# A recurrent-memory attention kernel: where the first half's row sums and the filler matmuls stand in a segment

## The chip, the cores and the metric

The kernel runs on one core of one Trainium2 chip. The time is device microseconds from start to end of one execution. Three executions of the kernel before took 1645.75, 1645.52 and 1643.44 us, so the median is 1645.52 us. A core has five engines that run side by side and wait for each other by semaphores: PE (TensorE: matmuls; its weight loads are shown apart as PEld), DVE (VectorE), ACT (ScalarE), POOL (GpSimd) and SP (SyncE, which here only issues DMAs). PE reads from SBUF and writes to PSUM, of which there are eight banks of 512 float32 columns.

## The reference, cut to what matters

Two layers, each of an attention block with a recurrent memory (A) and a gated feed-forward block (B), are run twice over 2048 rows of 512 columns. Only A is touched:

```python
mem = mem0                                   # 8 rows
for s in range(n_seg):                       # 2048 / 32 = 64 segments
    xs = x[:, s * seg_len:(s + 1) * seg_len, :]
    h = jnp.concatenate([mem, xs], axis=1)   # 8 + 32 = 40 rows
    q, k, v = (jnp.einsum('btd,dhe->bhte', h, W) for W in (Wq, Wk, Wv))   # 32 heads of 128
    scores = jnp.einsum('bhqe,bhke->bhqk', q, k) * scale
    p = softmax(where(mask, scores, -1e9))
    o = jnp.einsum('bhqk,bhke->bhqe', p, v)
    o = jnp.einsum('bhte,hed->btd', o, Wo)
    mem = o[:, :M, :]                        # the next segment needs these 8 rows
    outs.append(o[:, M:, :])
```

Each segment's memory rows are computed from the segment before, so 64 segments run one after another, in each of two layers: 128 in all. The softmax is not divided out on the scores: the kernel keeps E = exp(scores) times the mask, and divides the product of E and the values by the sums of E over the keys.

## The kernel before, in words

`segment` (L887) emits one segment. The order on PE, DVE and ACT is the order in which the program emits the instructions; POOL and SP are ordered by the framework.

**Heads and halves.** The 32 heads are handled in two halves, r = 0 and 1, of 16 heads each. For each half there are projections of Q and K (`qk`), a cast of the result by ACT (L904), a turn by DVE's 32x32 transposes (L907, into QQ and KA), scores on PE (`scores`, L930 and L934, into psS), an exponential on ACT (`exps`, L939), and a product with the mask on DVE (`close`, L942, into E). E has 128 partitions: four groups of 32 keys, where a group holds every fourth head; the mask writes each score row twice with zeros where another head stands, so that one contraction over 64 partitions serves two groups. The new values are cast to VA by ACT (L1018, half 0) and DVE (L1027, half 1).

**Tiles of the array.** Most matmuls use the array as four tiles of 128 rows and 32 columns (`tile_position=(0, 32 * cg)`), so that four matmuls run side by side, each writing 32 partitions of PSUM. The products with the values (`pv`, L973 and L976, into psO[r]) and the sums (`sums_memory` L956, `sums_tokens` L965) use it as two tiles of 64 rows and 128 columns: g is the pair of key groups on partitions 64g to 64g + 63.

**Sums and outputs.** `sums_memory(r, ps, fresh)` sums E over the keys for the queries that are memory rows: four matmuls with a matrix of ones, two of them over a second part of E that holds the segment-end rows (`e_own`). For r = 0 the sums go to psT (two banks, shared in time with psS and psQ under the tag "att"), for r = 1 to columns 320 to 383 of psO[1]. `memory_out(r, ps)` takes the logarithm (L990) and the exponential of its negative (L991) on ACT into Rm, and DVE multiplies psO[r]'s memory rows by it into uT (L992). `sums_tokens` fills psT with the sums for all other queries, which are inverted later in Rt (L1054, L1057) and used by `tok_out` and `last_out` (L995, L998).

**Wo.** `wo_pairs` (L773, into px) takes heads 0 to 19 from uT and so needs half 0's memory rows first, and half 1's from head 16 on; `wo_rest` (L780) takes heads 20 to 31 into columns 384 to 511 of psO[0]. `fold` and `build_hA` (L869 to L879) add the pieces and turn them into the next segment's first rows of hT, with which its projections (psQ) begin. psQ also waits until Rt's logarithm (L1054) has read psT.

**Fillers.** Work that is off this chain is handed out in pieces by a generator, `more`; `fill()` asks it for the next piece. In three segments of four it is `b_units`: full passes of 16 matmuls (four k-tiles by four column tiles) that project the last 8 rows of each segment of the next 128-row block (hB) into psb. A pair of passes is given out as three pieces: k-tiles 0 to 2 of the first (12 matmuls), its k-tile 3 (4 matmuls), and the whole second pass (16). In the other segment, from the fifth block on, it is `y_part`, a piece of Wo for those rows (pwB), split in the same way; in the first four blocks that segment has no filler. So a layer has four such segments without fillers, eight in all. Finished passes are cast by ACT (L758) and turned by a DMA on SP (L763), both issued by `run(copies)`.

The three calls of `fill()` in a segment stand behind `close(1)`, behind `memory_out(1)`, and behind `last_out(0)`. What PE sees of it is: scores of half 1; 12 filler matmuls; `sums_memory(0)`; `pv(0)`; `pv(1)`; `sums_memory(1)`; `sums_tokens`; 4 filler matmuls; `wo_pairs`; `wo_rest`; 16 filler matmuls; the next segment. The first segment of the first layer takes its fillers elsewhere.

Of the kernel before, what the change touches and what calls it, by code (L numbers as in the profile page):

```python
# [7 lines left out]
BF16 = mybir.dt.bfloat16  # L8
# [6 lines left out]
P = 128  # L15
# [38 lines left out]
def _consts(ctx, tc, c, b_sp):  # L54
    nc = tc.nc
    cp = ctx.enter_context(tc.tile_pool(name="consts", bufs=1))
    bsp = cp.tile([P, 16], F32, name="bsp")
    tctx = ExitStack()
    tmp = tctx.enter_context(tc.tile_pool(name="consts_tmp", bufs=1))
    ident_f = tmp.tile([P, P], F32, name="ident_f")  # L60
    nc.gpsimd.memset(ident_f[:], 0.0)
    nc.gpsimd.affine_select(out=ident_f[:], in_=ident_f[:], compare_op=ALU.not_equal, fill=1.0,
                            base=0, pattern=[[-1, P]], channel_multiplier=1)
    ident_bf = cp.tile([P, P], BF16, name="ident_bf")
    nc.vector.tensor_copy(ident_bf[:], ident_f[:])


    maskf = tmp.tile([P, 224], F32, name="maskf")
    nc.gpsimd.memset(maskf[:], 1.0)
    fourth = tmp.tile([P, 4, 32], F32, name="fourth")  # L70
    nc.gpsimd.memset(fourth[:], 0.0)
    nc.gpsimd.affine_select(out=fourth[:], in_=fourth[:], compare_op=ALU.not_equal, fill=1.0,
                            base=0, pattern=[[-1, 4], [-4, 32]], channel_multiplier=1)
    own = maskf[:, 160:224].rearrange("p (i q) -> p i q", i=4)
    is_own = tmp.tile([P, 4, 1], F32, name="is_own")
    nc.vector.tensor_reduce(out=is_own[:], in_=fourth[:], op=ALU.max, axis=mybir.AxisListType.X)
    nc.vector.tensor_copy(own, is_own[:].to_broadcast([P, 4, 16]))
    for q in range(0, P, 32):
        blk = maskf[q:q + 32, 0:160].rearrange("p (i q) -> p i q", i=4)[:, :, 8:32]
        nc.gpsimd.affine_select(out=blk, in_=blk, compare_op=ALU.is_ge, fill=0.0, base=8,  # L80
                                pattern=[[0, 4], [1, 24]], channel_multiplier=-1)
        last = own[q:q + 32, :, 8:16]
        nc.gpsimd.affine_select(out=last, in_=last, compare_op=ALU.is_ge, fill=0.0, base=0,
                                pattern=[[1, 4], [4, 8]], channel_multiplier=-1)
    maskN = cp.tile([P, 2, 224], BF16, name="maskN")
    nc.vector.memset(maskN[:], 0.0)
    for gs in range(4):
        nc.vector.tensor_copy(maskN[32 * gs:32 * gs + 32, gs % 2, :], maskf[32 * gs:32 * gs + 32, :])
    ones = cp.tile([P, P], BF16, name="ones")
    nc.vector.memset(ones[:], 1.0)  # L90
    bsp_bf = cp.tile([P, 16], BF16, name="bsp_bf")

    def load_bsp():
        nc.vector.memset(bsp_bf[:], 0.0)
        nc.sync.dma_start(bsp_bf[:], b_sp.rearrange("(t p) -> p t", p=P))
        return lambda: nc.vector.tensor_copy(bsp[:], bsp_bf[:])

    c["bsp"], c["load_bsp"] = bsp, load_bsp
    tctx.close()
    c.update(ident_bf=ident_bf, maskN=maskN, ones=ones)  # L100
    return c


# [549 lines left out]
def a_block(tc, c, rows, front, MV_in, RS_in, MV_out, RS_out, ahead, wo, S, first):  # L653
    nc = tc.nc
    NSEG = S // SEG
    NB = S // P
    scale = float(DH) ** -0.5
    maskN, ones = c["maskN"], c["ones"]

    with ExitStack() as ctx:  # L660

# [74 lines left out]
        def b_units(tb, early=0):  # L736
            bs = blk_state[tb]
            order = (0, 2, 1, 3, 4, 5) if early else (4, 5, 0, 2, 1, 3)

            for k, j in enumerate(order):  # L740
                now = k < early
                ps = (accB if now and k % 2 and j != 5 else accA).tile([P, 512], F32, name="psb")[:]
                for kts in (((0, 1, 2), (3,)), ((0, 1, 2, 3),))[k % 2]:
                    mm_chunk(ps, lambda kt, cg: bs["hB"][:, kt, :],
                             lambda kt, cg: qk_rhs(w, j, kt, cg) if j < 4 and now else cols_rhs(w, j, kt, cg), kts)
                    if kts[-1] != KT - 1:
                        yield

                def out(k=k, j=j, ps=ps, now=now):
                    if j >= 4:  # L750
                        nc.scalar.copy(bs["VB"][:, :, j - 4, :], ps.rearrange("p (i e) -> p i e", i=4))
                        if now:
                            ahead.regroup(bs["VB"], bs["VX"], (j - 4,))
                        elif j == 5:
                            store_v(bs)
                        return
                    r = rowsB[:, k % 2, :]
                    nc.scalar.copy(r, ps)  # L758
                    t = bs[("QTB", "KTB")[j // 2]][:, j % 2]
                    if now:  # L760
                        turns.append(lambda: nc.vector.transpose(out=t.rearrange("p a b -> p (a b)"), in_=r))
                    else:
                        nc.sync.dma_start_transpose(out=t.rearrange("p (i g) k -> p i (g k)", g=4), in_=r.rearrange("t (i e) -> t i e", i=4))  # L763

                copies.insert(len(copies) if now else 0, out)
                yield
# [29 lines left out]
        def y_part(G, q, last=False):  # L796

            groups = [oBs[G][:, :, 32 * g:32 * g + 32] for g in range(4)]
            if last:
                parts = [[(groups[g], 8 * q + k) for g in range(3)] + [(groups[q], 24 + k)] for k in range(8)]  # L800
            else:
                parts = [[(groups[g], 8 * q + k) for g in range(4)] for k in range(8)]
            pwB = accA.tile([P, DM], F32, name="pwB")
            for k, _ in enumerate(wo_last(parts, pwB)):
                if k in (2, 3):
                    yield

            def add(lo, n, src):
                nc.vector.tensor_tensor(out=yB[G][lo:lo + n, :], in0=pwB[src:src + n, :], in1=yB[G][lo:lo + n, :], op=ALU.add)

            def out():
                n = 96 if last else P
                if q == 0:
                    yB[G] = wk.tile([P, DM], F32, name="yB", bufs=1)
                    nc.vector.tensor_copy(yB[G][0:n, :], pwB[0:n, :])
                else:
                    add(0, n, 0)
                if last:
                    if q == 2:
                        store_last(G, 0, 64, nc.sync)  # L820
                    add(32 * q, 32, 96)
                    if q == 2:
                        store_last(G, 64, 96, nc.sync)
                elif q == 3 and G < NB // 4 - 2:
                    stores.append(lambda: store_last(G, 0, P, nc.sync))
                elif q == 3:
                    store_last(G, 0, P, nc.sync)

            adds.append(out)
            yield  # L830
# [56 lines left out]
        def segment(s, fill, spare1, spare2, spare3, tail, loads):  # L887
# [11 lines left out]
            E = segp.tile([P, 2, 2, 224], BF16, name="E", bufs=1)  # L899
# [44 lines left out]
            def e_all(e, lo, hi):  # L944

                return e[:, :, 0:160].rearrange("p n (i q) -> p n i q", q=40)[:, :, :, lo:hi]

            def e_own(e, b):
                return e[:, :, 160:224].rearrange("p n (i b e) -> p n i b e", i=4, b=2)[:, :, :, b, :]

            def sums_memory(r, ps, fresh):

                for k in range(2):
                    for g in range(2):
                        e = E[64 * g:64 * g + 64, r]
                        nc.tensor.matmul(ps[:, g, :], lhsT=ones[64 * g:64 * g + 64, :], rhs=e_own(e, 0) if k else e_all(e, 0, 8),  # L956
                                         start=(fresh and k == 0), stop=True, skip_group_check=True)

            def sums_tokens(ps):

# [69 lines left out]
            psO = [attO[r].tile([P, 2, 512], F32, name="psO") for r in range(2)]  # L1030
            Rm = segp.tile([P, 2, 2, 64], F32, name="Rm", bufs=1)
            psT = att.tile([P, 2, 512], F32, name="psT")
            sums = (psT[:, :, 0:64], psO[1][:, :, 320:384])
            if not (first and s == 0):
                fill()
            sums_memory(0, sums[0], True)
            pv(0)
            memory_out(0, sums[0])
            spare1(E)
            pv(1)  # L1040
            sums_memory(1, sums[1], False)
            sums_tokens(psT)
            memory_out(1, sums[1])
            if not (first and s == 0):
                fill()
            run(copies)
            px = accB.tile([P, 512], F32, name="px")
            wo_pairs(px, uT_cur)
# [43 lines left out]
        start = nc.vector if first else nc.gpsimd  # L1092
# [114 lines left out]
        for i in range(H // 2):  # L1207
            for k in range(4):
                h = 2 * i + k % 2
                nc.tensor.matmul(pw[32 * k:32 * k + 32, :], lhsT=ends[k // 2][:, h, :], rhs=wo.head(h).rearrange("p (kt g el) -> p g kt el", kt=4, g=4),  # L1210
                                 start=(i == 0), stop=(i == H // 2 - 1), tile_position=(0, 32 * k))
# [46 lines left out]
```

## Time and profile before

| what | value |
|---|---|
| median of three runs (1643.44 to 1645.75) | 1645.52 us |
| profiled execution, its own time | 1643.32 us |
| its span (first to last instruction) | 1641.6 us |
| granted TensorE clock, mean | 0.997 |
| busy: PE / PEld / DVE / ACT / POOL | 97% / 58% / 74% / 65% / 18% |
| segments, psQ to psQ: usual | 10.10 to 10.20 us |
| segment without fillers | 10.10 us |
| two feed-forward blocks, from the last segment's start on | 159 us, and the span's last 153 us |

The profile is one execution taken by the hardware profiler. The times of all rows are microseconds from the span's start. A matmul's row runs from its start to a modelled end, so rows of PE overlap; the distance between starts tells how long a group takes on the array. A row of weight loads (PEld) can begin ahead of its matmuls. What stands in brackets behind a row is the idle time of the engine ahead of it, and what ended it.

### The profile page before, as it was taken

Reading aid. Unit: us, or ns where it says so; the run is one execution under the profiler, and the core shown is the slowest. Engines: PE = TensorE matmul, PEld = TensorE weight load, DVE = VectorE, ACT = ScalarE, POOL = GpSimd, SP = SyncE. Lnnn points to the kernel's source line nnn. Section 1 sums busy time; section 2 is a strip of 40 time slices with the busy share of each in tenths; the row PEclk is TensorE's granted clock in tenths of the full one; section 3 lists DMA queues with packets and bytes.
Section 4 is the critical chain, followed back from the end, with each engine's and each line's share of the span. In section 5 each row is a group of like instructions: output and inputs, shape, how many; then the busy total and the mean of one; then the engine's idle time right before and its main releaser. Section 6 shows DMA issues by size and latency. Waiting matters only on the chain.

```text
span 1641.6 us, 86352 instructions
## 1 busy us (share of the span) xinstructions
PE 1585.8 (97%) x38610; PEld 953.5 (58%) x38610; DVE 1207.2 (74%) x3176; ACT 1074.9 (65%) x2278; POOL 290.0 (18%) x604
## 2 busy tenths in 40 slices
PE   3899999999999999999999999999999999999999
PEld 1455556555565556566655555665565666565565
DVE  3677777778887887884467777777788778878722
ACT  2577777777777777661047777777777777776400
POOL 5111111112211222320011111111122112214000
PEclk9999999999999999999999999999999999999999
DMA  9322111113321233276952222222233223435697
GB/s 354 101 42 42 42 42 44 44 42 74 81 57 42 76 89 79 87 180 154 215 163 46 50 48 45 46 46 45 57 92 84 46 59 95 100 60 156 150 194 166
DMA packets 264731, 148.99 MB, mean 91 GB/s; under 512 B 198680, under 2 KB 240784, under 8 KB 264360
## 3 DMA queue, kind: packets, MB, share of 16 engines
q1 hardware_dynamic: 251128, 99.66, 27.8%
q0 software_dynamic: 13232, 43.82, 8.3%
q8 instruction: 302, 4.95, 1.3%
q14 instruction: 69, 0.57, 0.1%
HBM read 59.68 MB, written 37.19 MB: 59 GB/s over the span
## 4 chain that ended last, share of the span: by engine, by line
PE 55%; DVE 2%; ACT 1%; issue 0%; DMA 0%; DVEq 0%
PE pg L388 9%; PE psQ L697 7%; PE psK L697 7%; PE psb L697 5%; PE px L773 4%; PE pz L287 4%; PE psV L697 3%; PE psm L697 3%; PE psO L780 2%; PE py L431 2%; PE psO L973 2%; PE pwB L792 1%; PE psT L965 1%; PE psS L930 1%; PE psT L956 1%; PE pw L1210 0%
## 5 line engine op out<-in xcount | busy, mean ns | idle before, releaser
L697 PEld LDWEIGHTS <-hT 128*32 128x32 bf16 x12288 | 328.6, 96 | 318.6 <-DVE hT L879 84.2
L907 DVE STREAM_TRANSPOSE QQ<-rows 128x512 bf16<-128x512 bf16 x256 | 179.5, 701 | 16.8 <-ACT rows L904 11.8
L907 DVE STREAM_TRANSPOSE KA<-rows 128x512 bf16<-128x512 bf16 x256 | 175.3, 685 | 11.5 <-ACT rows L904 8.7
L388 PE MATMUL pg<-z,wspT 128*128 128x344 bf16 x1024 | 154.3, 309 | 0.0
L904 ACT CAST rows<-psQ 128x512 bf16<-128x512 f32 x256 | 140.9, 585 | 17.1 <-PE psQ L697 16.9
L995 DVE TENSOR_TENSOR uT<-psO,Rt 128x384 bf16<-128x384 f32 x256 | 141.1, 551 | 12.4 <-ACT Rt L1057 8.1
L1057 ACT ACTIVATE Rt<-Rt 128x512 f32<-128x512 f32 x256 | 147.2, 622 | 4.1
L697 PE MATMUL psQ<-Wq_sb,hT 128*32 128x512 bf16 x2048 | 135.3, 383 | 11.2 <-ACT Rt L1054 6.0
L939 ACT ACTIVATE S<-psS 128x224 bf16<-128x224 f32 x256 | 91.4, 357 | 81.3 <-PE psS L934 81.2
L992 DVE TENSOR_TENSOR uT<-psO,Rm 128x128 bf16<-128x128 f32 x256 | 74.5, 291 | 93.2 <-ACT Rm L991 85.8
L773 PEld LDWEIGHTS <-uT 128*32 128x32 bf16 x5120 | 125.3, 96 | 26.9 <-DVE uT L992 13.3
L773 PE MATMUL px<-Wo,uT 128*32 128x256 bf16 x3840 | 134.5, 274 | 1.1 <-DMA Wo<-in_A_Wo_dram 0.2
L697 PE MATMUL psQ<-Wk_sb,hT 128*32 128x512 bf16 x2048 | 134.5, 380 | 0.0
L697 PE MATMUL psK<-Wv_sb,hT 128*32 128x512 bf16 x2048 | 134.2, 379 | 0.0
L697 PE MATMUL psm<-Wq_sb,hT 128*32 128x512 bf16 x2048 | 134.2, 379 | 0.0
L697 PE MATMUL psK<-Wk_sb,hT 128*32 128x512 bf16 x2048 | 134.2, 379 | 0.0
L697 PE MATMUL psV<-Wv_sb,hT 128*32 128x512 bf16 x2048 | 133.6, 378 | 0.0
L1054 ACT ACTIVATE Rt<-psT 128x1024 f32<-128x1024 f32 x128 | 131.1, 1024 | 3.2
L388 PEld LDWEIGHTS <-wspT 128*128 128x128 bf16 x1024 | 100.2, 98 | 53.2
L863 POOL COPY KX<-old 128x128 bf16<-128x128 bf16 x128 | 69.1, 548 | 304.5 <-PE psS L934 243.5
L863 POOL COPY KX<-front 128x128 bf16<-128x128 bf16 x126 | 66.8, 546 | 293.7 <-PE psS L934 226.0
L697 PEld LDWEIGHTS <-hB 128*32 128x32 bf16 x2976 | 70.1, 96 | 81.3 <-issue 30.4
(192 smaller groups left out, 2949.4 us busy)
## 6 DMA issues: line engine op xcount, KB each, us to landing
o_d<-o_sb SPq DMA_DIRECT2D x126, 64.0 KB
vb_d<-front SPq DMA_DIRECT2D x30, 256.0 KB
VX<-vb_d SPq DMA_DIRECT2D x120, 64.0 KB
ln_x<-xd SPq DMA_DIRECT2D x26, 256.0 KB
y_o<-o_d POOLq DMA_DIRECT2D x22, 256.0 KB, 3.4
xd<-y_o POOLq DMA_DIRECT2D x22, 256.0 KB, 3.0
Wq_sb<-in_A_Wq_dram POOLq DMA_DIRECT2D x8, 512.0 KB, 9.2
Wk_sb<-in_A_Wk_dram POOLq DMA_DIRECT2D x8, 512.0 KB, 11.0
```

What stands on the lines that cost most here:

```text
L287: nc.tensor.matmul(pz[:, c0:c1], lhsT=xnT[:, kt, :], rhs=w_in_sb[:, kt, c0:c1], start=(kt == 0), stop=(kt == KT - 1))
L388: nc.tensor.matmul(pg[t][:, k, 0:344], lhsT=wsp[t][:, st, :], rhs=z(st, 344 * k, 344 * k + 344), start=(st == 0), stop=(st == NT - 1))
L697: return [nc.tensor.matmul(ps[32 * cg:32 * cg + 32, :], lhsT=lhs(kt, cg), rhs=rhs(kt, cg), start=(kt == 0), stop=(kt == KT - 1), tile_posi ...
L773: nc.tensor.matmul(px[at:at + 32, 0:256], lhsT=lhs[:, h, :], rhs=wo_rhs(h, slice(k + 2, None, -2) if h % 2 else slice(k, None, 2)), start= ...
L863: eng.tensor_copy(KX[:, :, r].rearrange("p g (k i) -> p i g k", i=4), bs["KTB"][:, r].rearrange("p (i g) k -> p i g k", i=4)[:, :, :, 8 * ...
L904: return r, mms, nc.scalar.copy(r[:], ps)
L907: nc.vector.transpose(out=QQ[:, j % 2, :, 0:32] if j < 2 else KA[:, j % 2], in_=r[:])
L939: return nc.scalar.activation(out=S[:, r], in_=psS[:, r, 0:224], func=ACT.Exp, scale=scale)
L992: nc.vector.tensor_tensor(out=hview(uT_cur[:], r, 24, 32), in0=oview(r, 0, 8), in1=rm.rearrange("p g (n q) -> p g n q", q=8), op=ALU.mult)
L995: nc.vector.tensor_tensor(out=hview(uT_nxt[:], r, 0, 24), in0=oview(r, 8, 32), in1=rview(r, 0, 24), op=ALU.mult)
L1054: nc.scalar.activation(out=Rt[:], in_=psT[:], func=ACT.Ln)
L1057: nc.scalar.activation(out=rt, in_=rt, func=ACT.Exp, scale=-1.0)
```

## The change

`sums_memory` now serves half 1 alone. For half 0 there is `sums_ahead`: sixteen matmuls on 128x32 tiles, which is the tile form of the fillers. They contract over all 128 partitions with a constant, `half`, that is one on 64 partitions and zero on the other 64, so that each g gets the same sums as before. They write the two g side by side into columns 384 to 511 of psO[1]'s first bank, and no longer into psT. They are emitted behind the first filler piece and ahead of the second.

The calls of `fill()` stand behind `close(1)`, behind `sums_ahead`, and, as before, behind `last_out(0)`; the one between `memory_out(1)` and `run(copies)` is gone. The first pass is split as k-tile 0 (4 matmuls) and k-tiles 1 to 3 (12), and `y_part` yields at 0 and 3 in place of 2 and 3. So PE sees: scores of half 1; 4 filler matmuls; `sums_ahead` (16 small ones); 12 filler matmuls; `pv(0)`; `pv(1)`; `sums_memory(1)`; `sums_tokens`; `wo_pairs`; `wo_rest`; 16 filler matmuls. The semaphore waits that the changed program has and the one before had not: the first matmul of `sums_ahead` waits for DVE's E of half 0, `pv(1)` waits for ACT's L1003 (the logarithm of half 0's sums, L990 before), and `sums_tokens` no longer waits for that logarithm.

```diff
--- before.py
+++ after.py
@@ -88,6 +88,10 @@
         nc.vector.tensor_copy(maskN[32 * gs:32 * gs + 32, gs % 2, :], maskf[32 * gs:32 * gs + 32, :])
     ones = cp.tile([P, P], BF16, name="ones")
     nc.vector.memset(ones[:], 1.0)
+    half = cp.tile([P, 2, 32], BF16, name="half")
+    nc.vector.memset(half[:], 0.0)
+    for g in range(2):
+        nc.vector.memset(half[64 * g:64 * g + 64, g, :], 1.0)
     bsp_bf = cp.tile([P, 16], BF16, name="bsp_bf")
 
     def load_bsp():
@@ -97,7 +101,7 @@
 
     c["bsp"], c["load_bsp"] = bsp, load_bsp
     tctx.close()
-    c.update(ident_bf=ident_bf, maskN=maskN, ones=ones)
+    c.update(ident_bf=ident_bf, maskN=maskN, ones=ones, half=half)
     return c
 
 
@@ -655,7 +659,7 @@
     NSEG = S // SEG
     NB = S // P
     scale = float(DH) ** -0.5
-    maskN, ones = c["maskN"], c["ones"]
+    maskN, ones, half = c["maskN"], c["ones"], c["half"]
 
     with ExitStack() as ctx:
 
@@ -740,7 +744,7 @@
             for k, j in enumerate(order):
                 now = k < early
                 ps = (accB if now and k % 2 and j != 5 else accA).tile([P, 512], F32, name="psb")[:]
-                for kts in (((0, 1, 2), (3,)), ((0, 1, 2, 3),))[k % 2]:
+                for kts in (((0,), (1, 2, 3)), ((0, 1, 2, 3),))[k % 2]:
                     mm_chunk(ps, lambda kt, cg: bs["hB"][:, kt, :],
                              lambda kt, cg: qk_rhs(w, j, kt, cg) if j < 4 and now else cols_rhs(w, j, kt, cg), kts)
                     if kts[-1] != KT - 1:
@@ -802,7 +806,7 @@
                 parts = [[(groups[g], 8 * q + k) for g in range(4)] for k in range(8)]
             pwB = accA.tile([P, DM], F32, name="pwB")
             for k, _ in enumerate(wo_last(parts, pwB)):
-                if k in (2, 3):
+                if k in (0, 3):
                     yield
 
             def add(lo, n, src):
@@ -948,13 +952,22 @@
             def e_own(e, b):
                 return e[:, :, 160:224].rearrange("p n (i b e) -> p n i b e", i=4, b=2)[:, :, :, b, :]
 
-            def sums_memory(r, ps, fresh):
+            def sums_memory(r, ps):
 
                 for k in range(2):
                     for g in range(2):
                         e = E[64 * g:64 * g + 64, r]
                         nc.tensor.matmul(ps[:, g, :], lhsT=ones[64 * g:64 * g + 64, :], rhs=e_own(e, 0) if k else e_all(e, 0, 8),
-                                         start=(fresh and k == 0), stop=True, skip_group_check=True)
+                                         start=False, stop=True, skip_group_check=True)
+
+            def sums_ahead(ps):
+
+                e = E[:, 0]
+                for g in range(2):
+                    for k in range(2):
+                        for cg in range(4):
+                            nc.tensor.matmul(ps[32 * cg:32 * cg + 32, g, :], lhsT=half[:, g, :], rhs=e_own(e, 0) if k else e_all(e, 0, 8),
+                                             start=(g == 0 and k == 0), stop=True, tile_position=(0, 32 * cg), skip_group_check=True)
 
             def sums_tokens(ps):
 
@@ -1030,19 +1043,19 @@
             psO = [attO[r].tile([P, 2, 512], F32, name="psO") for r in range(2)]
             Rm = segp.tile([P, 2, 2, 64], F32, name="Rm", bufs=1)
             psT = att.tile([P, 2, 512], F32, name="psT")
-            sums = (psT[:, :, 0:64], psO[1][:, :, 320:384])
+            sums = (psO[1][:, 0, 384:512].rearrange("p (g n) -> p g n", g=2), psO[1][:, :, 320:384])
             if not (first and s == 0):
                 fill()
-            sums_memory(0, sums[0], True)
+            sums_ahead(sums[0])
+            if not (first and s == 0):
+                fill()
             pv(0)
             memory_out(0, sums[0])
             spare1(E)
             pv(1)
-            sums_memory(1, sums[1], False)
+            sums_memory(1, sums[1])
             sums_tokens(psT)
             memory_out(1, sums[1])
-            if not (first and s == 0):
-                fill()
             run(copies)
             px = accB.tile([P, 512], F32, name="px")
             wo_pairs(px, uT_cur)
```

## The prediction

> **What bounds the kernel now.** The first view is the page: the engines' busy shares and the chain that ended last.
>
> ```profile
> span 1641.6 us, 86352 instructions
> PE 1585.8 (97%) x38610; PEld 953.5 (58%) x38610; DVE 1207.2 (74%) x3176; ACT 1074.9 (65%) x2278; POOL 290.0 (18%) x604
> PE 55%; DVE 2%; ACT 1%; issue 0%; DMA 0%; DVEq 0%
> ```
>
> PE carries the chain, but "97% busy" is not "97% useful": a matmul's row includes its trip through the array. What counts is when each group of matmuls starts, so the second view is the timeline of one segment, 267.81 to 277.98 us (128 such segments run one after another, nearly all within 10.1 to 10.3 us). Columns: start, duration, engine, line, tile written and read, count.
>
> ```profile
> 272.92 0.39 DVE L942 TENSOR_TENSOR E<-S,maskN 128x448 bf16<-128x448 bf16 x1
> 273.12 0.28 PE L930 MATMUL psS<-QQ,KA 128*32 128x40 bf16 x16
> 273.22 0.21 PE L934 MATMUL psS<-QQ,KX 128*32 128x64 bf16 x4
> 273.25 0.83 PE L697 MATMUL psb<-Wq_sb,hB 128*32 128x512 bf16 x12
> 273.55 0.36 ACT L939 ACTIVATE S<-psS 128x224 bf16<-128x224 f32 x1 [0.19 <-PE psS L934]
> 273.96 0.38 DVE L942 TENSOR_TENSOR E<-S,maskN 128x448 bf16<-128x448 bf16 x1
> 274.01 0.23 PE L956 MATMUL psT<-E,ones 64*128 64x64 bf16 x4
> 274.08 0.31 PE L973 MATMUL psO<-E,VA 64*128 64x80 bf16 x8
> 274.22 0.22 PE L976 MATMUL psO<-E,VX 64*128 64x128 bf16 x2
> 274.40 0.32 PE L973 MATMUL psO<-E,VA 64*128 64x80 bf16 x8
> 274.59 0.24 PE L956 MATMUL psO<-E,ones 64*128 64x64 bf16 x4
> 274.65 0.45 PE L965 MATMUL psT<-E,ones 64*128 64x512 bf16 x4
> 274.94 0.29 DVE L992 TENSOR_TENSOR uT<-psO,Rm 128x128 bf16<-128x128 f32 x1 [0.60 <-ACT Rm L991]
> 275.03 0.40 PE L697 MATMUL psb<-Wq_sb,hB 128*32 128x512 bf16 x4
> 275.29 1.05 PE L773 MATMUL px<-Wo,uT 128*32 128x256 bf16 x30
> 275.52 0.29 DVE L992 TENSOR_TENSOR uT<-psO,Rm 128x128 bf16<-128x128 f32 x1 [0.28 <-ACT Rm L991]
> 276.39 0.84 PE L780 MATMUL psO<-Wo_high,uT 128*32 128x128 bf16 x48
> 277.06 1.03 PE L697 MATMUL psb<-Wk_sb,hB 128*32 128x512 bf16 x16
> 277.98 0.62 PE L697 MATMUL psQ<-Wq_sb,hT 128*32 128x512 bf16 x8
> ```
>
> See three things. Starts on PE give prices: full passes of 16 matmuls by 512 columns start 0.86 apart (269.54, 270.40 and 271.26 earlier in this segment), so four of them cost 0.216 us; sixteen score matmuls cost 0.10 (273.12 to 273.22); four by 64 columns cost 0.03. There are idle places: pv(0) (274.08, 274.22) needs 0.175, so it is over at 274.26, yet pv(1) starts at 274.40, 0.06 after E's second half is closed (273.96 + 0.38 = 274.34). And Wo's pairs start at 275.29, 0.06 after uT's first half (274.94 + 0.29 = 275.23), while the filler ahead of them was over at 275.03 + 0.22 = 275.25. The third view, the list of waits, has the same second wait over the whole span, and in the eight segments without fillers it reaches 0.5 us (the weight loads feel it first):
>
> ```profile
> PEld L773 <- DVE uT L992: 13.3, 71, 0.5
> PEld L956 <- issue: 55.1, 128, 0.5
> ```
>
> Its other row is the turn from 32-column tiles to 64-row tiles, once a segment on L956 (0.43 on the weight loads; on the matmuls 0.11: the twelve fillers end at 273.25 + 0.65 = 273.90, L956 starts at 274.01). The turn back is 0.09 to 0.11: L965 needs 0.216 + 0.055 from 274.65, and the filler starts at 275.03.
>
> **From Wo's start to the next segment nothing changes.** From 275.29 to the next psQ at 277.98 stand px, its copies (cross), Rt's logarithm and build_hA, none of them touched; psQ starts 0.05 after Rt's first step has left psT, and PE's sixteen fillers end 0.05 before that. ACT and DVE all hang on px there, so this stretch moves as a block. Ahead of it, from psQ to 273.25, PE streams without a gap. So the change is worth what it does between the first filler (273.25) and Wo's start (275.29): 2.04 us now.
>
> **The change, part by part.** I count PE starts from 273.25.
>
> 1. The first half's four sums (L956 on psT) go: minus 0.07 (274.01 to 274.08). Sixteen matmuls of 64 columns on 32-column tiles come. The trace has no row with this operand, but L934 is the same form (128x32 tile, 64 columns, runs of eight): 0.03 for four, so 0.12 for sixteen. Floor: the 40-column L930 row, 0.10. Ceiling: 0.03 each if they go one after another, 0.48. I take L934's, the nearest in form, but its four matmuls stream four different operands and the new ones the same one. The Trainium skill (TensorEngine Tiling (Array Packing), Instruction Overhead) speaks against the change here: about 60 cycles of overhead for each matmul, which at the 2.4 GHz of its page TensorE: Matmul & The Clock Gate would be an estimated 0.40 us for the sixteen. By that the segment would lose 0.15; the trace disagrees for four tiles side by side, with sixteen started in 0.10.
>
> 2. Fillers: 4 + 12 ahead of the values in place of 12 ahead and 4 behind; the same 16 matmuls, 0.86 in all, and the third chunk of 16 stays. What they issue besides is nothing: the cast of psb (L758) and its DMA transpose on SP are issued by run(copies), which keeps its place behind Exp(1) on ACT; POOL and SP keep their order. The y_part chunks (yield at 0 and 3 instead of 2 and 3) follow the same split.
>
> 3. The stall before pv(1) goes. New order: four fillers 0.22, sums 0.34, twelve fillers 0.99, turn 1.10, pv(0) 1.275: PE is ready for pv(1) at 274.53, while E is closed at 274.34. Minus 0.14.
>
> 4. New waits. The sums wait for E's first half (272.92 + 0.39 + 0.06 = 273.37; PE gets there at 273.47): hidden by 0.10; behind them on PE stand twelve fillers. pv(1) now waits until Ln(0) has read its sums out of psO[1], one tile with pv(1)'s output; behind it stands all of PE. Ln(0) is freed from pv(0)'s company: it follows the exponential (273.55 + 0.36) and takes 0.28, so it ends at 274.22 + 0.05: hidden by 0.26.
>
> 5. The cover between the last sums and Wo goes. pv(1) 0.19, sums 0.06, tokens and turn 0.38: Wo could start at 273.25 + 1.905 = 275.16. It needs uT's first half. Exp(0) now ends about 274.6, so the values release it: pv(0) starts at 274.35, its last pair starts 0.14 later and takes 0.22, 0.05 to DVE, 0.29, 0.06 to PE: 275.11. Covered by 0.04. The second half: its sums come 0.125 later than now, so uT at 275.81 + 0.125 + 0.06 = 276.00, and the pairs reach head 16 eight groups of 0.11 behind their start, 276.04. Covered by 0.04 as well. The wait of 0.04 that stood before Wo goes.
>
> Sum: -0.07 - 0.14 - 0.04 + 0.12 = -0.13 us in 119 segments, 15.5 us. In the eight without fillers (tb up to 3, fourth segment, both blocks) L965 starts at 81.68 and Wo at 82.25 (the first block's fourth segment); 0.38 behind L965 is 82.06, and uT's first half is then ready at about 81.96: -0.19 each, 1.5 us. Segment 0 waits for Wo's DMA, at no gain. The three memsets at the start lie beside the weight loads: nothing; uncovered, under 0.3. The feed-forward blocks are untouched. Together 17 us: span 1641.6 to 1624.6, the profiled execution's 1643.3 to 1626.3. The median of the runs, 1645.5, lies 2.2 above that execution, though their lowest, 1643.4, does not; I put the time at 1627.
>
> **Rivals.**
>
> A is the forecast, 1622 to 1632: sums at 0.10 and the longer stalls of some segments (up to 0.25 before pv(1)) make 21 us, sums at 0.145 some 12.
>
> B: a new wait before Wo or at head 16. Both margins are 0.04. For it: DVE also runs statistics and row work between the two products. Against: that work stands behind the first product, which now comes earlier. If either is 0.04 to 0.10 beyond its margin, 0.09 to 0.03 of the 0.13 remain: 11 to 4 us, so 1633 to 1640.
>
> C, slower: the sixteen sums do not run side by side, because four tiles stream one operand. 0.48 for 0.12 is +0.36 - 0.13 = +0.23 in 119 segments, less 1.5: +26, so 1670. It decides from 0.25 us for the sixteen, 16 ns each. Against: every 32-column row in the trace starts its four tiles 3 to 5 ns apart. By the skill's overhead rule (same page and section), 0.40, the time would be near 1660; the trace disagrees, as said.
>
> D: no gain, because pv(1)'s start is handed from E to Ln(0). It would have to end 0.26 later than worked out, 1644 to 1647; the profile shows ACT free between the exponential and Ln(0).
>
> **The numbers.** A 0.72, B 0.15, C 0.09, D 0.04. So faster by over 0.2% (3.3 us, about what a measurement can tell from no change) 0.87, within 0.2% 0.04, slower 0.09. The range runs from A's best, with the runs' 2 us of spread, to B's end: 1620 to 1640.
>
> **What would show it.** Right: starts on PE from first filler to Wo about 1.9 us apart instead of 2.04, segments near 10.03; sixteen new matmuls in 0.12; pv(1) 0.18 behind pv(0); ACT's Ln(0) close behind the exponential; DVE's first product released by PE instead of ACT. Wrong: sixteen sums over 0.25 us; fillers held up behind them by E; a wait of PE on L992's uT that has grown; pv(1) waiting for ACT; psQ held by something that did not move with px.

## The result, and the profile after

The changed kernel takes 1636.43 us (median of four runs, 1634.92 to 1638.26) against 1645.44 for the kernel before, timed beside it: a ratio of 0.9940 [0.9928, 0.9952], so 9.0 us gained. The forecast was 1627, 18 us gained against the same median, in a range of 1620 to 1640. The profiled execution took 1634.92 us, span 1633.2, which is 8.4 less than the span before. The comparisons below are made between spans.

The page of the changed kernel; the last line is the larger of the two queues that the profile calls instruction (packets, MB, share of 16 engines), which had 302 packets and 4.95 MB before:

```profile
span 1633.2 us, 89437 instructions
PE 1576.7 (97%) x40146; PEld 966.0 (59%) x40146; DVE 1211.6 (74%) x3179; ACT 1062.0 (65%) x2278; POOL 292.0 (18%) x604
PE 54%; DVE 1%; ACT 1%; DMA 1%; issue 0%; SPq 0%; DVEq 0%
q8 instruction: 315, 5.16, 1.3%
```

The engines' shares say nothing of the gain. What the reader is to see is the count of matmuls, 38610 before and 40146 now: 1536 more, and as many weight loads. It comes up again below.

The timeline of the same segment as before, from the last scores to the next segment's psQ:

```profile
271.16 0.39 DVE L946 TENSOR_TENSOR E<-S,maskN 128x448 bf16<-128x448 bf16 x1
271.44 0.21 PE L938 MATMUL psS<-QQ,KX 128*32 128x64 bf16 x4
271.47 0.40 PE L701 MATMUL psb<-Wq_sb,hB 128*32 128x512 bf16 x4
271.68 0.30 PE L969 MATMUL psO<-E,half 128*32 128x64 bf16 x16
271.80 0.83 PE L701 MATMUL psb<-Wq_sb,hB 128*32 128x512 bf16 x12
272.05 0.28 ACT L1003 ACTIVATE Rm<-psO 128x128 f32<-128x128 f32 x1
272.18 0.38 DVE L946 TENSOR_TENSOR E<-S,maskN 128x448 bf16<-128x448 bf16 x1
272.56 0.32 PE L986 MATMUL psO<-E,VA 64*128 64x80 bf16 x8
272.77 0.31 PE L986 MATMUL psO<-E,VA 64*128 64x80 bf16 x8
272.97 0.22 PE L960 MATMUL psO<-E,ones 64*128 64x64 bf16 x4
273.03 0.44 PE L978 MATMUL psT<-E,ones 64*128 64x512 bf16 x4
273.05 0.29 DVE L1005 TENSOR_TENSOR uT<-psO,Rm 128x128 bf16<-128x128 f32 x1 [0.49 <-PE psO L989]
273.40 1.05 PE L777 MATMUL px<-Wo,uT 128*32 128x256 bf16 x30
273.89 0.29 DVE L1005 TENSOR_TENSOR uT<-psO,Rm 128x128 bf16<-128x128 f32 x1 [0.55 <-ACT Rm L1004]
276.09 0.48 PE L701 MATMUL psQ<-Wq_sb,hT 128*32 128x512 bf16 x4
```

Most of the signs that the prediction asked for are there. The sixteen new matmuls take 0.12 us (271.68 to 271.80). pv(1) starts 0.21 behind pv(0), as soon as PE is through with it: E was closed at 272.18 + 0.38 = 272.56, long before 272.77. Ln(0) (L1003) stands at 272.05 and is over at 272.33. DVE's first product is released by PE. From the first filler to Wo it is 1.93 us, 2.04 before. The segments are 10.06 us long instead of 10.165 (the median), not the 10.03 that was forecast. One sign of being wrong is there as well, a grown wait on uT before Wo.

Wo starts at 273.40 by two reasons at once: uT's first half (273.05 + 0.29 + 0.06 = 273.40), and the tokens' sums with the turn behind them (273.03 + 0.216 + 0.055 + 0.09 = 273.39). In the list of waits this shows as weight loads that wait for uT 124 times, 33.0 us in all, where it was 71 times and 13.3 before:

```profile
PEld L986 <- ACT Rm L1003: 50.5, 119, 0.4
PEld L777 <- DVE uT L1005: 33.0, 124, 0.6
PEld L784 <- issue: 4.8, 9, 2.1
```

The first row looks like a wait for Ln(0), and is not: Ln(0) ends at 272.33, and the loads begin at 272.56. It is the turn from 32-column to 64-row tiles, 0.42 each, which stood on `PEld L956 <- issue` before (55.1 us in 128 segments, 0.43 each). The third row has nine idle times ahead of Wo's rest (L784) for which no release is shown; before, its counterpart L780 had two. In both kernels the longest (2.1 and 2.2 us) falls in segment 0, where PE waits for Wo's DMA. So eight others of 0.17 to 0.85 us stand against one of 0.53. One of them:

```profile
183.84 1.12 PE L784 MATMUL psO<-Wo_high,uT 128*32 128x128 bf16 x48
184.67 0.12 PEld L784 LDWEIGHTS <-uT 128*32 128x32 bf16 x7 [0.23 <-issue]
184.78 1.05 PE L701 MATMUL psb<-Wk_sb,hB 128*32 128x512 bf16 x16
185.01 0.22 DVE L882 TENSOR_TENSOR memT<-psO,t 128x64 bf16<-128x64 f32 x1 [0.26 <-PE psO L784]
```

Elsewhere this group of 48 takes 0.84; here PE stands for some 0.28 before the last eight, and the next segment's rows (memT) wait with it. I call such a thing a pause: two matmuls of one group that start over 0.04 us later than usual after each other, while neither waits for a semaphore. Over the segments (63, 64 and 127, at the ends of the layers, left out) the kernel before has 4 pauses of 1.0 us in all, the changed one 13 of 2.6 us.

### The profile page after: what moved, and what is told of

It reads as the page before. It is cut to its first block, busy times and chain, and to the rows that moved or that the text cites. A ratio compares the mean times of both kernels' runs of the same rounds, so it can differ in the third digit from the quotient of the medians.

```text
span 1633.2 us, 89437 instructions
## 1 busy us (share of the span) xinstructions
PE 1576.7 (97%) x40146; PEld 966.0 (59%) x40146; DVE 1211.6 (74%) x3179; ACT 1062.0 (65%) x2278; POOL 292.0 (18%) x604
## 4 chain that ended last, share of the span: by engine, by line
PE 54%; DVE 1%; ACT 1%; DMA 1%; issue 0%; SPq 0%; DVEq 0%
PE pg L392 9%; PE psQ L701 7%; PE psK L701 7%; PE px L777 5%; PE psb L701 5%; PE pz L291 4%; PE psm L701 3%; PE psV L701 3%; PE psO L784 2%; PE py L435 2%; PE psO L986 2%; PE pwB L796 1%; PE psT L978 1%; PE psS L934 1%; PE pw L1223 0%; PE psO L969 0%
## 5 line engine op out<-in xcount | busy, mean ns | idle before, releaser
L701 PEld LDWEIGHTS <-hT 128*32 128x32 bf16 x12288 | 336.2, 96 | 310.8 <-DVE hT L883 81.6
L1005 DVE TENSOR_TENSOR uT<-psO,Rm 128x128 bf16<-128x128 f32 x256 | 74.6, 291 | 105.8 <-PE psO L989 56.7
L777 PEld LDWEIGHTS <-uT 128*32 128x32 bf16 x5120 | 117.5, 96 | 48.0 <-DVE uT L1005 33.0
L1003 ACT ACTIVATE Rm<-psO 128x128 f32<-128x128 f32 x256 | 71.1, 278 | 74.2 <-PE psO L960 74.2
```

Of the source, the lines that this page charges most:

```text
L701: return [nc.tensor.matmul(ps[32 * cg:32 * cg + 32, :], lhsT=lhs(kt, cg), rhs=rhs(kt, cg), start=(kt == 0), stop=(kt == KT - 1), tile_posi ...
L777: nc.tensor.matmul(px[at:at + 32, 0:256], lhsT=lhs[:, h, :], rhs=wo_rhs(h, slice(k + 2, None, -2) if h % 2 else slice(k, None, 2)), start= ...
L1003: nc.scalar.activation(out=rm, in_=ps, func=ACT.Ln)
L1005: nc.vector.tensor_tensor(out=hview(uT_cur[:], r, 24, 32), in0=oview(r, 0, 8), in1=rm.rearrange("p g (n q) -> p g n q", q=8), op=ALU.mult)
```

## The experiments

The theory after the result: the change does what it says; the missing 8 us are the pace of PE (pv(0) is longer than priced) and pauses, which come with the number of PE's instructions. Rivals: the missing part is scatter between executions; it is a new wait for uT before Wo (rival B of the prediction); the sums' price is paid elsewhere. Edits are against the changed kernel unless said otherwise. All times are medians; ratios are to the kernel before, run on the same chip (1644.3 to 1644.5).

**The same again.** First the changed kernel unchanged, then the one before.

> The changed kernel once more, unaltered, for a second profile. Of the 17 us forecast, 9 came. By the first profile a usual segment went from 10.16 to 10.06 us (12 us in 119 segments, 1.5 us in the eight without fillers), and some 5 us were lost again: 2.4 us in pauses of PE in mid-stream without a wait, 2.4 us in the two feed-forward blocks and the last segments, 0.6 us ahead of the first segment. Theory 1 (the losses come from PE's instruction stream: 12 more matmuls and weight loads in a segment, 24 x 128 = 3072 more instructions, so that PE runs dry more often): about 1636 us, again some 10 to 20 such pauses worth 2 to 4 us in the segments, at places that mostly recur because the stream is the same. Theory 2 (chance of one execution): pauses back at the level of the kernel before (6, 1.1 us), the feed-forward blocks 159.2 and 152.7 us long as before.

1636.34 us, 0.9948 [0.9931, 0.9964]; 11 pauses, 2.9 us, eight of them in segments where the first profile has one too (13, 31, 56, 57, 65, 99, 104, 113). The counterpart of the pause above, of this second execution:

```profile
184.63 0.29 PE L784 MATMUL psO<-Wo_high,uT 128*32 128x128 bf16 x8 [0.37 <-issue]
184.98 0.23 DVE L882 TENSOR_TENSOR memT<-psO,t 128x64 bf16<-128x64 f32 x1 [0.54 <-PE psO L784]
```

It is the same place, the last eight of the group, but 0.54 instead of 0.26 in front of memT. So most of the places belong to the program, the length to the execution. The first feed-forward block took 158.5 us here, 160.3 in the first profile, and 159.2 and 160.0 in the two profiles of the kernel before: that part was scatter.

> The kernel before, unaltered, for a second profile. Theory 1 (the losses come from the number of PE's instructions): few pauses of PE without a wait, as in its first profile (4, 1.0 us). Theory 2 (chance): 10 or more in this one.

1645.25 us in one run, 3 pauses of 0.5 us. The kernel before has few of them, again.

**One half of the change alone.** The new sums, but the fillers as before (twelve ahead of the sums, four behind `memory_out(1)`; `y_part` is split as before too):

```diff
-                for kts in (((0,), (1, 2, 3)), ((0, 1, 2, 3),))[k % 2]:
+                for kts in (((0, 1, 2), (3,)), ((0, 1, 2, 3),))[k % 2]:
...
             sums_ahead(sums[0])
-            if not (first and s == 0):
-                fill()
             pv(0)
...
             memory_out(1, sums[1])
+            if not (first and s == 0):
+                fill()
```

> Only the sums are changed (sixteen whole-height matmuls into psO[1], behind the twelve fillers); the fillers stay 12 ahead and 4 behind. Theory (the gain is one of order: it needs fillers between the sums and the values): the sums end 0.12 behind the twelve fillers, the logarithm of them reads psO[1] until about 0.5 later, and the second half's values wait for it, 0.18 later than they start now behind E: Wo 0.13 us later than before in 119 segments, about +16 us, 1655 to 1663. Rival (the tile form of the sums is what gains, since they follow the fillers without a turn of the array): 1630 to 1642, as the changed kernel.

1661.33 us, 1.0102 [1.0087, 1.0117]: 17 us slower than before. Its timeline:

```profile
275.79 0.83 PE L701 MATMUL psb<-Wq_sb,hB 128*32 128x512 bf16 x12
276.44 0.30 PE L969 MATMUL psO<-E,half 128*32 128x64 bf16 x16
276.67 0.32 PE L986 MATMUL psO<-E,VA 64*128 64x80 bf16 x8
276.80 0.28 ACT L1003 ACTIVATE Rm<-psO 128x128 f32<-128x128 f32 x1 [0.36 <-PE psO L969]
277.13 0.32 PE L986 MATMUL psO<-E,VA 64*128 64x80 bf16 x8
277.77 0.40 PE L701 MATMUL psb<-Wq_sb,hB 128*32 128x512 bf16 x4
277.99 0.28 PE L777 MATMUL px<-Wo,uT 128*32 128x256 bf16 x4
```

Now pv(1) does wait for Ln(0): 276.80 + 0.28 = 277.08, and pv(1) starts at 277.13, 0.46 behind pv(0) instead of 0.21. That is the wait of rival D, and twelve fillers between the sums and pv(0) are what keeps the changed kernel clear of it.

The fillers' new place alone, with the old sums (edit against the kernel before; `y_part` is split as in the changed kernel):

```diff
-                for kts in (((0, 1, 2), (3,)), ((0, 1, 2, 3),))[k % 2]:
+                for kts in (((0,), (1, 2, 3)), ((0, 1, 2, 3),))[k % 2]:
...
-                fill()
+                fill(2)
             sums_memory(0, sums[0], True)
...
             memory_out(1, sums[1])
-            if not (first and s == 0):
-                fill()
```

> Only the fillers are moved: all sixteen ahead of the values, none behind the last sums; the first half's sums stay four matmuls of 64 rows into psT, behind the sixteen. Theory: the stall of the second half's values goes as in the changed kernel, but the chain sums, logarithm, exponential, product now starts behind all sixteen fillers and ends 2.25 us behind the first filler, where Wo starts at 2.04 before and 1.93 in the changed kernel: +0.21 us in 119 segments, about +25 us, 1665 to 1674. Rival (the gain is the removed stall and the removed sums, and Wo's cover did not matter): 1632 to 1640.

1670.18 us, 1.0155 [1.014, 1.017]: 26 us slower than before. Its timeline:

```profile
277.01 1.05 PE L697 MATMUL psb<-Wq_sb,hB 128*32 128x512 bf16 x16
277.99 0.23 PE L956 MATMUL psT<-E,ones 64*128 64x64 bf16 x4
278.26 0.28 ACT L990 ACTIVATE Rm<-psT 128x128 f32<-128x128 f32 x1 [0.60 <-PE psT L956]
278.57 0.31 ACT L991 ACTIVATE Rm<-Rm 128x128 f32<-128x128 f32 x1
278.59 0.45 PE L965 MATMUL psT<-E,ones 64*128 64x512 bf16 x4
278.91 0.29 DVE L992 TENSOR_TENSOR uT<-psO,Rm 128x128 bf16<-128x128 f32 x1 [0.81 <-ACT Rm L991]
279.26 0.40 PE L773 MATMUL px<-Wo,uT 128*32 128x256 bf16 x8 [0.22 <-DVE uT L992]
```

With the sums behind all sixteen fillers, the logarithm, the exponential and the product follow one another, and Wo, with no filler ahead of it any more, waits for their end (278.91 + 0.29 + 0.06 = 279.26). So the two halves cost 17 and 26 us by themselves and gain 8 together: the early sums are what lets the fillers go ahead, and the fillers are what hides Ln(0).

**Some cover kept before Wo.** Four fillers ahead of the sums, eight behind them, four before Wo:

```diff
-                for kts in (((0,), (1, 2, 3)), ((0, 1, 2, 3),))[k % 2]:
+                for kts in (((0,), (1, 2), (3,)), ((0, 1, 2, 3),))[k % 2]:
...
             memory_out(1, sums[1])
+            if not (first and s == 0):
+                fill()
```

(`y_part` and the counts of pieces follow.)

> The changed kernel with the fillers split 4 + 8 ahead of the values and 4 behind the last sums, so that Wo's start has its cover again. Theory A (PE's own stream and the turn of the array set Wo's start; the second half's values would stand 0.06 us behind E again): Wo 0.06 us later in 119 segments, +7 us on 1636.4, so 1641 to 1645. Theory B (PE waits for the first half's uT at Wo, and a cover gives that back): 1629 to 1636.

1642.61 us, 0.9981 [0.9972, 0.999]. Here uT is ready 0.27 before Wo starts, so no wait for it is left, and still the kernel is 6 us slower than the changed one. Rival B, as an account of the missing gain, falls: to give Wo's wait its cover back gains nothing. The starts say why: the group behind the tokens' sums follows them by 0.366 in the median segment of both kernels, a filler here and Wo there, so the turn alone holds Wo that long. The 6 us can be read off the timeline:

```profile
273.34 0.62 PE L701 MATMUL psb<-Wq_sb,hB 128*32 128x512 bf16 x8
273.70 0.38 DVE L946 TENSOR_TENSOR E<-S,maskN 128x448 bf16<-128x448 bf16 x1
273.89 0.32 PE L986 MATMUL psO<-E,VA 64*128 64x80 bf16 x8
274.14 0.32 PE L986 MATMUL psO<-E,VA 64*128 64x80 bf16 x8
274.38 0.29 DVE L1005 TENSOR_TENSOR uT<-psO,Rm 128x128 bf16<-128x128 f32 x1 [0.30 <-PE psO L989]
275.00 1.04 PE L777 MATMUL px<-Wo,uT 128*32 128x256 bf16 x30
```

E is closed at 273.70 + 0.38 = 274.08, and pv(1) starts 0.06 later: the stall that the change removed is back by 0.04 here, and by 0.06 in the median segment, which is 7 us in 119. Four fillers fewer stand ahead of it.

**Another place for the sums among the fillers.** Eight fillers ahead, eight behind (`y_part` follows):

```diff
-                for kts in (((0,), (1, 2, 3)), ((0, 1, 2, 3),))[k % 2]:
+                for kts in (((0, 1), (2, 3)), ((0, 1, 2, 3),))[k % 2]:
```

> The changed kernel with the first pass split 8 + 8: eight fillers, sums, eight fillers, values. Theory (PE's stream alone sets Wo's start; the first half's logarithm must have read its sums by 1.31 us behind the first filler, and does so 1.10 behind it here instead of 0.91): no change, 1635 to 1637.5. Rival (the values wait for the logarithm, or the later exponential reaches Wo): 1640 to 1650.

1635.57 us, 0.9953 [0.9939, 0.9966]: the same as the changed kernel. Ln(0) ends at 272.55 in this segment and pv(1) starts at 272.78: as long as that order holds, moving the sums by four fillers changes nothing.

**The sums' price.** First twice over:

```diff
             sums_ahead(sums[0])
+            sums_ahead(sums[0])
```

> The changed kernel with the sixteen sums issued twice (the second time overwrites the first). It prices the step that was disputed. Theory 1 (four side by side, 0.115 us for sixteen as the first profile shows, all of it on the path in 119 segments, hidden behind E in the eight without fillers): +13.7 us on about 1636, so 1650; with 4096 more instructions on PE's stream the pauses without a wait grow by another 2 to 4 us: 1651 to 1654. Theory 2 (the pauses are chance): 1649 to 1651, with as many pauses as in the run beside it. Theory 3 (part of the sums is hidden, because the first half's product and not PE sets Wo's start): 1637 to 1646.

1658.2 us, 21.9 more than the changed kernel, where the array time of sixteen matmuls (0.115 in 119 segments, 13.7 us, and a little for the rest) was to give 15 to 18. The list of waits has the difference in the same row as above (its longest, 2.3, is segment 0's DMA again):

```profile
PEld L784 <- issue: 10.4, 19, 2.3
```

The segments have 31 pauses of 8.6 us now. Of 32 that I found over the whole span, 27 end 1.1 to 1.5 us after a packet of 16 KB landed on the instruction queue, whose packets land about every 4.1 us here. To tell the array's time from the number of instructions, the sums were then made wider: eight matmuls of 128 columns in place of sixteen of 64, and sixteen of 128. These two kernels leave the own rows out of the first half's sums and add the two pairs of groups into one another, so they serve for timing alone.

```diff
-                    for k in range(2):
+                    for k in range(1):
                         for cg in range(4):
-                            nc.tensor.matmul(ps[32 * cg:32 * cg + 32, g, :], lhsT=half[:, g, :], rhs=e_own(e, 0) if k else e_all(e, 0, 8),
+                            nc.tensor.matmul(psO[1][32 * cg:32 * cg + 32, 0, 384:512], lhsT=half[:, g, :], rhs=e_all(e, 0, 16),
```

> The changed kernel with eight sums of 128 columns in place of sixteen of 64: the same time on the array (two starts of four at 0.055 against four at 0.028), but 16 instructions fewer in a segment. The own rows are left out of the first half's sums and both pairs of groups are added into one another, so the output is not the reference's. Theory 1 (pauses from the number of instructions): the pauses fall from some 12 (2.7 us) to the level of the kernel before, with 584 instructions in a segment against its 576: 1632 to 1634.5. Theory 2 (chance, or the sums' place alone): 1635.5 to 1637.

1632.54 us, 0.9925 [0.9911, 0.994]. The eight take 0.11 us on the array, as the sixteen did, and there are 1024 matmuls fewer: 3.9 us less than the changed kernel (the two ratios' intervals overlap, so the size is rough), 7 pauses of 0.9 us instead of 13 of 2.6.

> Sixteen sums of 128 columns: twice the time on the array, as in the run with the sums issued twice (1658.2), but with the changed kernel's number of instructions. The same parts of the sums are left out or added into one another. Theory 1: of that run's +21.9 us, 13.7 were array time and some 8 were pauses from 32 more instructions in a segment; so here 1648 to 1652. Theory 2 (sixteen more matmuls cost more on the array than their starts show): 1655 to 1660.

1645.62 us, 1.0008 [1.0, 1.0017]; with `range(2)` in place of `range(1)`. Less than expected: 13.1 over the eight, where 0.11 in 119 segments is 13.1 already, so eight more matmuls and weight loads a segment cost too little to be seen at this rate (10 pauses, 1.8 us). The pair that tells most is this one and the doubled sums: nearly as much time on the array (0.222 us a segment here, 0.231 there, by the starts), 16 matmuls and 16 weight loads fewer a segment, 12.6 us less. In the two profiles the segments differ by 9.3 us: 6.8 are pauses, and some 2.0 are 0.017 in each of 119 segments, for the sums and the twelve fillers behind them. From the last segment's start on they differ by another 4.3, which is taken up below. All profiles in order of the rate (matmuls and weight loads together; the same three segments left out of the pauses):

| kernel | PE's instructions a segment | per us | median segment, us | pauses, us in all |
|---|---|---|---|---|
| new place of the fillers alone | 576 | 55.5 | 10.38 | 0 |
| sums on 64-column tiles (below) | 584 | 56.7 | 10.30 | 1, 0.06 |
| before | 576 | 56.7 | 10.165 | 4, 1.0 |
| before, again | 576 | 56.7 | | 3, 0.5 |
| eight wide sums | 584 | 58.1 | 10.05 | 7, 0.9 |
| new sums alone | 600 | 58.1 | 10.32 | 5, 0.6 |
| sixteen wide sums | 600 | 59.0 | 10.16 | 10, 1.8 |
| some cover kept | 600 | 59.2 | 10.13 | 12, 2.0 |
| changed kernel | 600 | 59.7 | 10.06 | 13, 2.6 |
| the same, again | 600 | 59.7 | | 11, 2.9 |
| eight and eight around the sums | 600 | 59.7 | | 12, 2.6 |
| sums twice | 632 | 61.9 | 10.21 | 31, 8.6 |

The pauses go with the rate, not with the count: the new sums alone have as many instructions as the changed kernel, in longer segments, and 0.6 us of pauses. That it is the fetch of instructions that PE pauses for is an inference, from the landings and from this order; no run changed the fetch itself.

**Fewer instructions in another tile form.** The sums on two tiles of 64 columns, eight matmuls in place of sixteen:

```diff
-    half = cp.tile([P, 2, 32], BF16, name="half")
+    half = cp.tile([P, 2, 64], BF16, name="half")
...
-                        for cg in range(4):
-                            nc.tensor.matmul(ps[32 * cg:32 * cg + 32, g, :], lhsT=half[:, g, :], rhs=e_own(e, 0) if k else e_all(e, 0, 8),
-                                             start=(g == 0 and k == 0), stop=True, tile_position=(0, 32 * cg), skip_group_check=True)
+                        for cg in range(2):
+                            nc.tensor.matmul(ps[64 * cg:64 * cg + 64, g, :], lhsT=half[:, g, :], rhs=e_own(e, 0) if k else e_all(e, 0, 8),
+                                             start=(g == 0 and k == 0), stop=True, tile_position=(0, 64 * cg), skip_group_check=True)
```

> The changed kernel with its sums on two tiles of 128 rows and 64 columns: eight matmuls of 64 columns for sixteen, the same four starts of 0.028 us, 16 instructions fewer in a segment, the same sums. Theory T (it is the tile form of the fillers that makes the sums cheap there; every other form costs a turn of the array on each side, 0.09 to 0.11 us each by the rows at the values): +0.17 us in 119 segments, +20 us, less 2 to 4 us of pauses for the fewer instructions: 1651 to 1656. Rival (a turn is only paid between 64 and 128 rows, not between 32 and 64 columns): the array time of the changed kernel with fewer pauses, 1631 to 1634, which would be the fastest of all.

1660.46 us, 1.0098 [1.0084, 1.0111]: 24 us slower than the changed kernel, some 5 more than the most that was expected. Its timeline:

```profile
275.56 0.40 PE L701 MATMUL psb<-Wq_sb,hB 128*32 128x512 bf16 x4
275.89 0.32 PE L969 MATMUL psO<-E,half 128*64 128x64 bf16 x8
276.14 0.83 PE L701 MATMUL psb<-Wq_sb,hB 128*32 128x512 bf16 x12
```

Four fillers take 0.22, so PE was free at 275.78 and the sums start 0.11 later; from there to the next filler it is 0.25, of which the eight take 0.147 (their starts) and the way back 0.10. So a turn is paid between 32 and 64 columns as well, and 0.11 + 0.10, with the 0.03 that the eight take beyond the sixteen, is 0.24 us in a segment, 10.30 against 10.06. The Trainium skill (TensorEngine Tiling (Array Packing), Key Properties) says that a change of the tiling mode drains the TensorE. The trace agrees, with about 0.1 us lost each way here. The sums are cheap in the changed kernel because they have the fillers' form.

## Why the prediction was right in direction and 9 us off

The time lies within the range, but in rival B's part of it (1633 to 1640) and not in that of its rival A, the forecast (1622 to 1632). B's sign is there, the grown wait on uT; its cause is not, as the run with the cover kept shows. That the range held is luck in this respect.

By its steps. The segments without fillers came out as forecast: 10.10 to 9.91, minus 0.19 in eight of them, 1.5 us. The usual ones gave 0.1075 in 119, 12.8 us, instead of 0.13, 15.5.

Step 1, the sums: right, 0.115 for the sixteen against the 0.12 taken. Rival C, one operand on four tiles, is refuted by the same rows. So is the 0.40 us that the prediction worked out from the Trainium skill (TensorEngine Tiling (Array Packing), Instruction Overhead) by adding up 60 cycles for each of the sixteen: four tiles run side by side, 0.028 us for each four, and the measurement decides.

Step 2, "what they issue besides is nothing": right as to the fillers. What the account left out is the new sums' own issue. They add twelve matmuls and twelve weight loads to each segment, and their number was priced at nothing; only the array's time was.

Step 3, the stall before pv(1): gone as said, but the term was mis-sized. It used 0.175 for pv(0), put together from the widths; the pair with VX (64 rows, 128 columns) takes 0.055 where 0.03 was set, and pv(0) takes 0.21. So the stall before was 0.12 us and not 0.14: its pair stood at 274.22 and was through at 274.28, and pv(1) started at 274.40. With the stall gone PE runs through it, so the error counts in full. From the first filler to Wo: forecast 1.905, measured 1.928; 0.023 in 119 segments is 2.7 us. (The other terms differ by 0.02 at most, and nearly cancel.)

Step 4, the new waits: both hidden, as said, and Ln(0) by 0.4 rather than 0.26. The run with the new sums alone shows the price when the cover is gone.

Step 5, the cover before Wo: the margin of 0.04 came out as zero, since uT and the tokens' sums end together. It cost nothing measurable: the turn holds what follows the tokens' sums for 0.366 with and without that wait, and with the cover given back the kernel was slower.

Of the 8.6 us between the 17.0 forecast and the 8.4 in the span, 2.7 are this mis-sized pace. Some 2.5 more are pauses (1.6 of the segments, 0.85 in the last one), tied to the instructions added: sixteen wide sums took 12.6 us less than thirty-two narrow ones of nearly the same array time. The first segment starts 0.6 later (psQ at 32.40, 31.77 before). Nine profiles with `half` have it at 31.9 to 33.0, the three without at 30.8 to 31.8; why a microsecond goes there stays open, since the memsets of `half` (on DVE at 26.4, 0.22 us) are not on the path that releases psQ. The remaining 2.8 lie in the feed-forward blocks, the last segment and a few odd segments, and only part of it is scatter. Segment 64 takes 10.1 or 11.8 us in profiles of one kernel; in the longer case the granted clock is about half at its start (0.57 from 841 to 844.5 in the second profile of the changed kernel).

From the last segment's start to the end it is 152.75 us in both profiles before, but 154.1 and 156.8 in the two of the changed kernel. The two have a pause in the last segment's Wo rest (0.85 and 1.42 us), which neither profile before has. Behind the longer one the granted clock fell as well. The rows give a stretch, its length, the busy time of PE, PEld, DVE, ACT and POOL, the granted clock (share of full speed), and the DMA share with GB/s; the first is of the second profile, the other of the first:

```profile
1492.40:1495.80 3.40, 3.40 (x36) 1.55 (x38) 3.30 (x9) 0.00 (x0) 0.00 (x0) 0.52 0.35 116
1493.00:1496.00 3.00, 3.00 (x62) 1.57 (x54) 2.90 (x8) 0.00 (x0) 0.59 (x2) 1.00 0.56 193
```

The run with the sums twice has a pause of 2.09 us in the same group and a granted clock of 0.50 from 1513 to 1518; from the last segment's start on it takes 158.1 us, against 153.7 with sixteen wide sums, whose pause there is 1.04. Four profiles with pauses of 0.84 to 1.04 there, that one among them, show no such fall. So a long pause can be followed by more loss than its own length. That it brings the fall about was not tested.

From the span to the time itself it is 1.7 us before and after, as taken. The last 0.8 of the 9.4 comes from the step to the median: it lies 1.5 above the profiled execution, where 0.7 was allowed.

## What to carry to other kernels

Two moves that each make a kernel slower can make it faster together: a sum goes early to free its readers, and the work that it lets past is what hides those readers; price the pair, and look for the row that each leaves uncovered alone. Small matmuls between matmuls of their own tile form cost their array time alone (0.115 us for sixteen here); on two tiles of 64 columns they cost a turn each way besides, with half as many of them. On an engine that hardly waits, count the instructions as well as the array time: half as many, twice as wide, were some 4 us faster at the changed kernel's rate and 12.6 with the sums doubled.

## What was not expected of the hardware

PE pauses in the middle of a group with nothing to wait for, mostly in Wo's 48 short matmuls, and at places most of which recur in the second profile of the changed kernel. At 55 to 57 instructions of PE per us there is at most 1 us of it over the segments, at 59.7 it is 2.6 to 2.9, at 61.9 it is 8.6. The ends follow the landing of a 16 KB packet of instructions by 1.1 to 1.5 us in 12 of 14 cases of the changed kernel and 27 of 32 with the sums twice. And the name that a weight load's idle time carries at a turn of the tile form can be that of an engine which was done 0.2 us before (`PEld L986 <- ACT Rm L1003`): the constant 0.42 in 119 segments tells that it is the turn. Last, the granted clock can fall to half deep inside a program that keeps PE 97% busy: 0.52 for 3.4 us and 0.50 for 5 us, in the last segment above.
